# Moving two weight loads and one due date in a fused attention and double MLP kernel

## The chip, the cores and the metric

The kernel runs on one core of a Trainium2 chip. The metric is the device time of one execution in microseconds (us), the median of several runs. Engines are named as in the profile: PE (TensorE) multiplies matrices, with PEld for its weight loads; DVE is VectorE, ACT is ScalarE, POOL is GpSimd, and SP is SyncE, which here only issues transfers. A transfer (DMA) is issued by SP or POOL, in the order of that engine's queue, and moved by 16 shared DMA engines.

## The reference

Three stages follow each other on 6016 tokens with 256 channels, all in float32.

```python
qn = q / (norm(q, axis=tokens) + 1e-6);  kn = k / (norm(k, axis=tokens) + 1e-6)
a  = softmax(kn.T @ qn / tau)             # 256 x 256, over channels
x  = v @ a                                # 6016 x 256
h  = x @ w1;  x = (h * sigmoid(1.702 h)) @ w2      # d_ff 2048
h  = x @ w3;  y = where(h > 0, h, exp(min(h, 0)) - 1) @ w4
```

## The kernel before, in words

A first phase reads q and k, sums up `kn.T @ qn` and takes the softmax. The matrix `a` is folded into the first weights, so that `x @ w1` needs v alone; the fold of w1 is done in four parts on PE (`fold_w1`), the first ahead of the main loop and the other three during it.

The main loop has two passes. Pass A is the first MLP and pass B the second. Each pass runs over six groups of tokens (five of 1024 and one of 896), and each group over eight units, one for 256 of the 2048 hidden columns. A unit is written (pass, group, unit), all counted from 0: (A,0,0) is the first of the 96. Its first product is done by a Strassen-like scheme with seven products, numbered 1 to 7 and issued in the order 1, 5, 6, 2, 7, 3, 4 (line L678). Each of the seven is three matmuls, because every float32 number is kept as a high and a low part. So a unit has 21 matmuls for its first product and 24 (L776) for its second product, which belongs to the unit before it: the second product of unit u is issued among the first products of unit u+1. ACT and DVE stand between the two: ACT copies one sum from bank to bank near the unit's start (L945, awaited by product 6) and another (L952), DVE adds (L956, awaited by product 7, and L966, awaited by product 4), and both compute the activation and its high and low parts (L708, L709, L741).

Beside this runs background work, in one list called `queue`. Each unit has eight places (`bg(0)` to `bg(7)`) where a step or two of it is issued: in group 0 of pass A 1, 2, 1, 2, ... steps, 12 in all, in the later groups of pass A one at each place. In that list stand:

- the conversion of the weights (`rounds`, `some`). A block of 512 columns is loaded raw, scaled by ACT (L202, L203: two passes), shifted, joined and given its sign by DVE (L207, L210, L213), and split into a high part by ACT (L245) and a low part by DVE (L251). The blocks go through in the order of the list `order`: w1 0, w1 1, w2 0, w1 2, w1 3, w2 1, w2 2, w1 4, w1 5, w2 3, w2 4, w1 6, w1 7, w2 5, w2 6, w2 7. They are staggered: round t scales block t+1 and ends block t-2 in its first step, joins block t and splits off the high part of block t-1 in its second, gives block t its sign in the third and shifts block t+1 in the fourth. `some(12, near)` takes twelve steps and goes on to the end of the round. w3 and w4 follow as `far`, and their results are stored to DRAM (`w3d`, `w4d`).
- the last parts of the folded w1 (`combine_w1`, six steps, L264 and L267 to L275),
- the turning of v for the next group (`blocks_v`, L378, two steps for each half of the group; the second half's load, sixteen small transfers on SP at L371, is issued when the first half is done),
- the operands of the next group of a pass (`operands`): seven operands, each made by ACT (L425) and DVE (L416, L429) and stored to DRAM by POOL (L431) in tiles that share four buffers, so that the last of the seven needs the buffer of the third.

`need(name, i)` forces steps of the conversion until block i is done, at the place where it is called. Before the change it is called at the start of unit (A,0,p) for w2 block p. The second product of unit (A,0,p) reads that block, and that product is issued in the unit that follows.

At the last unit of a group, each product is followed by `load_next`, which reloads the operand that the product has just read for the last time (L131, on SP). It does so only if the operands of the next group are marked as made; the mark is set for all seven at once at the end of `operands`. What isn't loaded then is loaded at the unit's end.

In the last group of pass A (group 5) the weights of pass B are loaded on SP at the ends of units: the first weights in four parts c (L1078, 1792 KB each) over the first weights of units 2c and 2c+1 of pass A, and the second weights p-1 (L1081, 512 KB each) over those of unit p-1. SP takes its instructions in the order written; each waits until the buffer's last reader on PE is done.

Ahead of the main loop the list `PACE1` takes 16 steps of the conversion.

Of the kernel before, what the change touches and what calls it, by code (L numbers as in the profile page):

```python
# [22 lines left out]
def kernel(  # L23
# [47 lines left out]
    NP = KF // 2  # L71
# [39 lines left out]
    XOP = {1: 0, 2: 1, 3: 2, 4: 3, 5: 4, 6: 5, 7: 6}  # L111
# [5 lines left out]
    def first_weights(kind, c):  # L117
        w_first[kind, c] = wts.tile([P, 2, 2, 7, P], F32R, tag=f"wA{c}", name=f"wA{kind}")
        return w_first[kind, c]

    def second_weights(kind, p):
        w_second[kind, p] = wts.tile([P, 2, 2, C], F32R, tag=f"wB{p}", name=f"wB{kind}")
        return w_second[kind, p]

    def x_tile(kind, b, i):
        x_t[kind, b, i] = xp.tile([P, 2, BANK], F32R, tag=f"x{i}", name=f"x{kind}")
        return x_t[kind, b, i]

    def load_x(kind, b, i):
        n = wid[b]  # L130
        nc.sync.dma_start(out=x_tile(kind, b, i)[:, :, :n].bitcast(F32), in_=xd[kind, b][:, i, :, :])  # L131
# [5 lines left out]
    def stage(shape, name):  # L137
        return stg.tile(shape, F32R, tag="st", name=name, bufs=4)
# [200 lines left out]
    def parts(n, work=near):  # L339
        while n:  # L340
            x = next(work, None)
            if x is None:
                return
            n -= not x

    def need(name, i):
        while state["done"] < place[name, i]:
            n = place[name, i]
            parts(1, near if n < NEAR - 1 else last_near if n < NEAR else far)
# [37 lines left out]
    made = set()  # L387
# [18 lines left out]
    def operands(kind, b, direct=False):  # L406

        n = wid[b]
        t = full.pop((kind, b))
        b11, b12 = (t[:, 0, i * n:(i + 1) * n] for i in range(2))  # L410
        b21, b22 = (t[:, 1, i * n:(i + 1) * n] for i in range(2))
        temp = {}

        def sub(i, x, y):
            temp[i] = stg.tile([P, BANK], F32, tag="t", name="tt", bufs=3)
            nc.vector.tensor_sub(temp[i][:, :n], x, y)  # L416

        def tgt(i):
            if direct:
                return x_tile(kind, b, i)  # L420
            return stage([P, 2, BANK], "xt")

        def hi(i, x):
            d = hold_t[i] = tgt(i)
            nc.scalar.copy(d[:, 0, :n], x)  # L425

        def lo(i, x):
            d = hold_t[i]
            nc.vector.tensor_sub(d[:, 1, :n], x, d[:, 0, :n].bitcast(F32))  # L429
            if not direct:  # L430
                nc.gpsimd.dma_start(out=xd[kind, b][:, i, :, :], in_=d[:, :, :n].bitcast(F32))  # L431

        hold_t = {}
        hi(0, b11)
        sub(4, b12, b11)
        yield False
        hi(1, b21)
        lo(0, b11)
        yield False
        hi(2, b22)  # L440
        lo(1, b21)
        yield False
        hi(4, temp[4][:, :n])
        sub(5, b22, temp[4][:, :n])
        yield False
        lo(2, b22)
        lo(4, temp[4][:, :n])
        yield False
        hi(5, temp[5][:, :n])
        sub(6, b22, b12)  # L450
        yield False
        hi(6, temp[6][:, :n])
        lo(5, temp[5][:, :n])
        yield False
        sub(3, b21, temp[5][:, :n])
        lo(6, temp[6][:, :n])
        yield False
        hi(3, temp[3][:, :n])
        yield False
        lo(3, temp[3][:, :n])  # L460
        made.add((kind, b))
        yield False
# [40 lines left out]
    with tc.manual_schedule():  # L503
        make_identity(nc, ident)

        with ExitStack() as st:
# [24 lines left out]
            for i, m in enumerate(CHUNKS):  # L531
# [22 lines left out]
                if i in (8, 9):  # L554
                    if i == 8:
                        full_tile("A", 0)
                    for c in range(KC):
                        transpose_v(0, i - 8, c, bank[4 + 2 * (i - 8) + c])
                    if i == 9:
                        v_ops = operands("A", 0, direct=True)  # L560
                elif i > 9:
                    parts([1, 1, 1, 0][i - 10], v_ops)
# [19 lines left out]
            for i in range(2):  # L582
                for c in range(KC):
                    x = i * KC + c
# [72 lines left out]
        loaded = set()  # L657

        def load_next(u, i):

            if u[2] < NP - 1 or u not in units[:-1]:
                return
            nxt = units[units.index(u) + 1][:2]
            if nxt in made and nxt + (i,) not in loaded:
                loaded.add(nxt + (i,))
                load_x(*nxt, XOP[i])

        def product(dst, i, u, start):
            product_(dst, i, u, start)
            load_next(u, i)  # L670
# [197 lines left out]
        def finish(kind, b):  # L868
            while (kind, b) not in made:
                background(1)  # L870
# [141 lines left out]
        def v_later(b, h):  # L1012
            if h == 0:
                if b > 1:
                    finish("B", b - 2)
                full_tile("A", b)
                queue.insert(1, blocks_v(b, 0))
            else:
                queue.insert(1, chain(blocks_v(b, 1), operands("A", b)))

        def some(n, work):

            safe = False
            while n > 0 or not safe:
                safe = next(work, None)
                if safe is None:
                    return
                if not safe:
                    n -= 1
                    yield  # L1030
# [10 lines left out]
        for b in range(NG):  # L1041
            if b + 1 < NG:
                plan_at(("A", b, 1), lambda b=b: load_v(b + 1, 0))
                plan_at(("A", b, 3), lambda b=b: v_later(b + 1, 0))
                plan_at(("A", b, 5), lambda b=b: v_later(b + 1, 1))
            nxt = units[units.index(("A", b, 7)) + 2]
            plan_at(nxt, lambda b=b: queue.append(operands("B", b)))

        for t in range(len(units) + 1):
            u = units[t] if t < len(units) else None  # L1050
            if u:
                kind, b, p = u
                if kind == "A" and b == 0 and p:
                    need("w2", min(p, NP - 1))
                if u == ("B", 0, 0):
                    passA.close()
                    tp = ctx.enter_context(tc.tile_pool(name="tpB", bufs=1))
                for f in plan.get(u, []):
                    f()
                if kind == "A":  # L1060
                    if b == 0:
                        queue.append(some(12, near) if p < 5 else some(12, last_near))
                    if b and p % 2 == 0:
                        queue.append(some(1, far))
            step(t)
            if u is None:
                break

            if p == NP - 1:
                nxt = units[t + 1] if t + 1 < len(units) else None  # L1070
                if nxt:
                    finish(*nxt[:2])
                    for i in (1, 5, 6, 2, 7, 3, 4):
                        load_next(u, i)
            if kind == "A" and b == NG - 1:
                if p % 2:
                    c = p // 2
                    nc.sync.dma_start(out=first_weights("B", c).bitcast(F32), in_=w3d[c])  # L1078
                if p:
                    need("w4", p - 1)  # L1080
                    nc.sync.dma_start(out=second_weights("B", p - 1).bitcast(F32), in_=w4d[p - 1])  # L1081
                if p == NP - 1:
                    need("w4", p)
            if u == ("B", 0, 0):
                nc.sync.dma_start(out=second_weights("B", NP - 1).bitcast(F32), in_=w4d[NP - 1])
# [29 lines left out]
```

## Time and profile before

| | us |
|---|---|
| median of 3 runs (lowest to highest) | 1082.22 (1078.76 to 1082.24) |
| the profiled execution | 1078.05 |
| its span | 1076.3 |
| PE busy | 1047.0 (97%) |
| DVE busy | 840.7 (78%) |
| ACT busy | 759.6 (71%) |
| POOL busy | 72.1 (7%) |
| mean DMA rate | 134 GB/s over 144.31 MB |

The times inside the span are counted from its start. Pass A's main loop runs from about 67 to 573 us, pass B from there to the end. In a row of a timeline the number ahead is the start, the next the length, and the bracket at the end tells how long the engine was idle before it and what ended that. `x6` is the number of instructions merged into the row. Matmuls overlap, so that the distance of two starts tells their rate and not the length of one. The granted clock is a share of 2.4 GHz; it has two levels, 1.2 and 2.4 GHz.

### The profile page before, as it was taken

Reading aid. Unit: us, or ns where it says so; the run is one execution under the profiler, and the core shown is the slowest. Engines: PE = TensorE matmul, PEld = TensorE weight load, DVE = VectorE, ACT = ScalarE, POOL = GpSimd, SP = SyncE. Lnnn points to the kernel's source line nnn. Section 1 sums busy time; section 2 is a strip of 40 time slices with the busy share of each in tenths; the row PEclk is TensorE's granted clock in tenths of the full one; section 3 lists DMA queues with packets and bytes.
Section 4 is the critical chain, followed back from the end, with each engine's and each line's share of the span. In section 5 each row is a group of like instructions: output and inputs, shape, how many; then the busy total and the mean of one; then the engine's idle time right before and its main releaser. Section 6 shows DMA issues by size and latency. Waiting matters only on the chain.

```text
span 1076.3 us, 13797 instructions
## 1 busy us (share of the span) xinstructions
PE 1047.0 (97%) x4808; PEld 873.5 (81%) x4808; DVE 840.7 (78%) x1366; ACT 759.6 (71%) x1423; POOL 72.1 (7%) x126
## 2 busy tenths in 40 slices
PE   8989989999999999999899999999999999999998
PEld 6867868888888888888798877887888788788897
DVE  5987785677776785675436999988998998989986
ACT  5778777667777777766557776777676777777675
POOL 0000010012211220120100100000000000000000
PEclk9999999999999999999999999999999999999999
DMA  9913255358548557535746124104204204203200
GB/s 341 371 41 77 59 184 193 116 186 280 195 176 286 199 184 253 171 139 178 270 176 259 43 78 151 25 1 144 32 1 138 38 1 137 40 1 120 40 1 35
DMA packets 124918, 144.31 MB, mean 134 GB/s; under 512 B 90224, under 2 KB 94416, under 8 KB 124336
## 3 DMA queue, kind: packets, MB, share of 16 engines
q1 hardware_dynamic: 108704, 84.05, 25.6%
q0 software_dynamic: 16144, 59.38, 14.9%
q8 instruction: 38, 0.62, 0.2%
q14 instruction: 32, 0.26, 0.1%
HBM read 86.25 MB, written 57.15 MB: 133 GB/s over the span
## 4 chain that ended last, share of the span: by engine, by line
PE 61%; issue 16%; DVE 12%; ACT 5%; POOL 3%; DMA 3%; SPq 0%; DVEq 0%; POOLq 0%; ACTq 0%
PE b L678 28%; PE b L776 28%; PE b L800 4%; DVE gg L730 2%; DVE ee L725 2%; DVE sq L523 1%; DVE g L741 1%; DMA qk<-in_k_dram 1%; DVE ob L834 1%; DMA xdB<-xt 1%; PE b L474 1%; POOL xdA L431 1%; ACT g L737 1%; POOL xdB L431 1%; DVE b L956 1%
## 5 line engine op out<-in xcount | busy, mean ns | idle before, releaser
L776 PE MATMUL b<-g,wBA 128*128 128x512 f32 (+1 forms) x1152 | 296.6, 386 | 1.7 <-DVE g L741 1.7
L678 PE MATMUL b<-xA,wAA 128*128 128x512 f32 (+1 forms) x1008 | 267.8, 389 | 9.7 <-ACT b L945 4.5
L678 PE MATMUL b<-xB,wAB 128*128 128x512 f32 (+1 forms) x1008 | 265.3, 387 | 1.9 <-DVE b L956 1.9
L776 PE MATMUL b<-g,wBB 128*128 128x512 f32 x960 | 252.3, 390 | 2.9 <-ACT g L737 1.8
L776 PEld LDWEIGHTS b<-g,wBA 128*128 128x128 f32 x1152 | 216.9, 188 | 42.9 <-DVE g L741 2.2
L678 PEld LDWEIGHTS b<-xA,wAA 128*128 128x128 f32 x1008 | 188.5, 189 | 50.7 <-ACT b L945 8.4
L678 PEld LDWEIGHTS b<-xB,wAB 128*128 128x128 f32 x1008 | 186.3, 188 | 40.0 <-DVE b L956 4.6
L776 PEld LDWEIGHTS b<-g,wBB 128*128 128x128 f32 x960 | 179.8, 188 | 43.4 <-ACT g L737 3.9
L737 ACT CAST g<-gg 128x512 fp32r<-128x512 f32 (+1 forms) x192 | 117.9, 614 | 114.2 <-DVE gg L730 110.1
L725 DVE SCALAR_TENSOR_TENSOR ee<-ee,th 128x512 f32<-128x512 f32 (+1 forms) x192 | 129.5, 674 | 28.2 <-ACT th L715 28.2
L708 ACT ACTIVATE g<-b 128x512 fp32r<-128x512 f32 (+1 forms) x144 | 84.9, 590 | 87.8 <-PE b L678 87.2
L956 DVE TENSOR_TENSOR b<-b,s 128x512 f32<-128x512 f32 (+1 forms) x96 | 65.9, 687 | 100.9 <-PE b L678 93.5
L741 DVE TENSOR_TENSOR g<-gf,g 128x512 fp32r<-128x512 f32 (+1 forms) x192 | 128.5, 674 | 16.0 <-ACT gf L709 15.8
L741 DVE TENSOR_TENSOR g<-gg,g 128x512 fp32r<-128x512 f32 (+1 forms) x192 | 129.4, 674 | 8.9 <-ACT g L737 4.4
L730 DVE SCALAR_TENSOR_TENSOR gg<-b,ee 128x512 f32<-128x512 f32 (+1 forms) x144 | 98.0, 681 | 5.0
L714 ACT ACTIVATE ee<-b 128x512 f32<-128x512 f32 (+1 forms) x144 | 84.4, 586 | 21.7 <-PE b L678 21.6
L709 ACT ACTIVATE gf<-b 128x512 f32<-128x512 f32 (+1 forms) x144 | 84.4, 586 | 2.9 <-DVE g L741 2.5
L966 DVE TENSOR_TENSOR c<-b,s 128x512 f32<-128x512 f32 (+1 forms) x96 | 64.7, 674 | 24.4 <-PE b L678 24.2
L715 ACT ACTIVATE th<-b 128x512 f32<-128x512 f32 (+1 forms) x144 | 83.8, 582 | 0.0
L952 ACT COPY s<-b 128x512 f32<-128x512 f32 (+1 forms) x96 | 56.2, 586 | 21.4 <-PE b L678 21.4
L945 ACT COPY b<-b 128x512 f32<-128x512 f32 (+1 forms) x96 | 56.0, 583 | 16.9 <-PE b L678 16.8
L565 PE MATMUL b<-qk 128*128 128x256 f32 x188 | 43.8, 391 | 5.4 <-DMA qk<-in_k_dram 5.2
(101 smaller groups left out, 840.8 us busy)
## 6 DMA issues: line engine op xcount, KB each, us to landing
xdB<-xt POOLq DMA_DIRECT2D x35, 512.0 KB, 3.5
xB<-xdB SPq DMA_DIRECT2D x35, 512.0 KB, 5.2
xdA<-xt POOLq DMA_DIRECT2D x28, 512.0 KB, 3.2
xA<-xdA SPq DMA_DIRECT2D x28, 512.0 KB, 6.3
wAB<-w3d SPq DMA_DIRECT2D x4, 1792.0 KB, 7.8
out_dram<-ob SPq DMA_DIRECT2D x160, 32.0 KB, 1.6
qk<-in_q_dram SPq DMA_DIRECT2D x9, 512.0 KB, 5.8
qk<-in_k_dram SPq DMA_DIRECT2D x9, 512.0 KB, 6.7
```

Of the source, the lines that this page charges most:

```text
L678: nc.tensor.matmul(dst[:, :n], w[:, wi, p % 2, WOP[i], :], x[:, xi, :n], start=(start and k == 0), stop=(k == 2), skip_group_check=True,)
L708: nc.scalar.activation(self.sl(ik)[0], h, AF.Gelu_apprx_sigmoid)
L709: nc.scalar.activation(t[:, :n], h, AF.Gelu_apprx_sigmoid)
L714: nc.scalar.activation(e[:, :n], h, AF.Exp)
L715: nc.scalar.activation(t[:, :n], h, AF.Tanh, scale=0.5)
L725: nc.vector.scalar_tensor_tensor(out=e[:, :n], in0=e[:, :n], scalar=1.0, in1=t[:, :n], op0=ALU.add, op1=ALU.mult,)
L730: nc.vector.scalar_tensor_tensor(out=g[:, :n], in0=h, scalar=0.0, in1=e[:, :n], op0=ALU.max, op1=ALU.min)
L737: nc.scalar.copy(self.sl(ik)[0], self.tmp[ik][:, :self.n])
L741: nc.vector.tensor_sub(lo, self.tmp.pop(ik)[:, :self.n], hi.bitcast(F32))
L776: nc.tensor.matmul(bank[a][:, :n], w[:, f, wi, d * P:(d + 1) * P], g[:, gi, k * n:(k + 1) * n], start=fresh((kind, b, a)), stop=(p == NP - ...
L956: nc.vector.tensor_add(bank[c][:, :n], bank[b][:, :n], s5[:, :n])
L966: nc.vector.tensor_add(c22[:, :n], bank[b][:, :n], s5[:, :n])
```

## The change

Three things are changed. The loads of pass B's first weights, until now at the ends of units 1, 3, 5 and 7 of pass A's last group, stand at the ends of units 3, 4, 5 and 7, each still ahead of that unit's load of second weights. An operand is marked as made as soon as its own store is issued, and `load_next` asks for the mark of that operand alone; the mark for the whole group stays. And w2 block p is due at the start of unit p+1 of group 0 and no longer at that of unit p; the last block is due at unit (A,1,0).

```diff
@@ operands: lo @@
             if not direct:
                 nc.gpsimd.dma_start(out=xd[kind, b][:, i, :, :], in_=d[:, :, :n].bitcast(F32))
+                made.add((kind, b, i))
@@ load_next @@
             nxt = units[units.index(u) + 1][:2]
-            if nxt in made and nxt + (i,) not in loaded:
-                loaded.add(nxt + (i,))
-                load_x(*nxt, XOP[i])
+            x = nxt + (XOP[i],)
+            if x in made and x not in loaded:
+                loaded.add(x)
+                load_x(*x)
@@ the loop over the units @@
                 if kind == "A" and b == 0 and p:
-                    need("w2", min(p, NP - 1))
+                    need("w2", p - 1)
+                if u == ("A", 1, 0):
+                    need("w2", NP - 1)
@@
             if kind == "A" and b == NG - 1:
-                if p % 2:
-                    c = p // 2
+
+                for c in {3: (0,), 4: (1,), 5: (2,), 7: (3,)}.get(p, ()):
                     nc.sync.dma_start(out=first_weights("B", c).bitcast(F32), in_=w3d[c])
```

## Rows read from the trace of the kernel before

**Rows 1.** The page's busy shares: busy us, share of the span, instructions.

```profile
PE 1047.0 (97%) x4808; PEld 873.5 (81%) x4808; DVE 840.7 (78%) x1366; ACT 759.6 (71%) x1423; POOL 72.1 (7%) x126
```

**Rows 2.** Busy time by stretch: pass A's first group and its fifth.

```profile
core 0: us, PE busy (x) PEld busy (x) DVE busy (x) ACT busy (x) POOL busy (x), PEclk, DMA share, GB/s
...
68.50:167.00 98.50, 91.03 (x393) 72.18 (x392) 78.52 (x140) 74.38 (x140) 5.77 (x10) 0.98 0.38 114
412.80:494.60 81.80, 81.80 (x361) 67.47 (x360) 54.56 (x90) 58.01 (x111) 12.43 (x20) 1.00 0.55 184
```

**Rows 3.** Timeline of PE at the start of unit (A,0,1).

```profile
77.88 0.73 PE L776 MATMUL b<-g,wBA 128*128 128x512 f32 x2 [1.73 <-DVE g L741]
...
79.14 0.84 PE L776 MATMUL b<-g,wBA 128*128 128x512 f32 x3
82.19 2.62 PE L678 MATMUL b<-xA,wAA 128*128 128x512 f32 x6 [2.20 <-ACT b L945]
```

**Rows 4.** Busy time by stretch, columns as in rows 2: around two long stops.

```profile
82.10:86.30 4.20, 4.11 (x11) 3.26 (x12) 2.79 (x6) 2.15 (x5) 0.00 (x0) 0.59 0.67 167
...
523.40:526.50 3.10, 3.02 (x9) 2.70 (x10) 2.41 (x5) 2.93 (x7) 0.84 (x2) 0.53 1.03 420
...
511.60:526.40 14.80, 11.72 (x51) 10.10 (x50) 9.13 (x16) 8.74 (x18) 3.20 (x6) 0.88 1.00 375
```

**Rows 5.** Timeline of ACT at the start of unit (A,0,1).

```profile
80.39 0.71 ACT L202 ACTIVATE raw<-raw 128x512 f32<-128x512 f32 x1
...
81.50 0.63 ACT L945 COPY b<-b 128x512 f32<-128x512 f32 x1
```

**Rows 6.** Timeline of PE: its other stops in pass A's first group.

```profile
107.92 1.67 PE L678 MATMUL b<-xA,wAA 128*128 128x512 f32 x6 [0.70 <-ACT b L945]
...
137.82 1.66 PE L678 MATMUL b<-xA,wAA 128*128 128x512 f32 x6 [0.95 <-DVE b L956]
...
146.47 1.66 PE L678 MATMUL b<-xA,wAA 128*128 128x512 f32 x6 [0.61 <-ACT b L945]
...
152.83 0.96 PE L678 MATMUL b<-xA,wAA 128*128 128x512 f32 x3 [0.60 <-DVE c L966]
...
158.53 1.66 PE L678 MATMUL b<-xA,wAA 128*128 128x512 f32 x6 [0.64 <-ACT b L945]
```

**Rows 7.** Timeline of DVE at the start of unit (A,0,5).

```profile
136.46 0.71 DVE L378 STREAM_TRANSPOSE vt<-v_raw 128x512 f32<-128x512 f32 x1 [5.51 <-DMA v_raw<-in_v_dram]
```

**Rows 8.** Timeline of SP: the sixteen loads of v's second half.

```profile
126.06 8.61 SPq L371 DMA_DIRECT2D v_raw<-in_v_dram  x16
```

**Rows 9.** Timeline of SP: the reloads of operands in unit (A,0,7).

```profile
155.88 9.42 SPq L131 DMA_DIRECT2D xA<-xdA  x7
```

**Rows 10.** Timeline of SP: pass B's first weights 0, second weights 0 and 1.

```profile
511.65 0.34 SPq L1078 DMA_DIRECT2D wAB<-w3d  x1
512.86 14.34 SPq L1081 DMA_DIRECT2D wBB<-w4d  x2
```

**Rows 11.** Timeline of POOL: stores of pass B's operands.

```profile
512.17 1.14 POOL L431 DMA_DIRECT2D xdB<-xt  x2 [1.74 <-DVE xt L429]
...
523.18 0.53 POOL L431 DMA_DIRECT2D xdB<-xt  x1 [6.93 <-DVE xt L429]
```

**Rows 12.** Timeline of ACT in unit (A,5,2).

```profile
521.54 0.62 ACT L425 CAST xt<-tt 128x512 fp32r<-128x512 f32 x1 [5.56 <-DMA xdB<-xt]
```

**Rows 13.** Timeline of PE in unit (A,5,2).

```profile
518.11 1.38 PE L678 MATMUL b<-xA,wAA 128*128 128x448 f32 x6
519.32 1.38 PE L776 MATMUL b<-g,wBA 128*128 128x448 f32 x6
523.48 1.49 PE L678 MATMUL b<-xA,wAA 128*128 128x448 f32 x3 [2.77 <-DVE c L966]
```

**Rows 14.** The page's transfers: KB each, median us to landing.

```profile
xdB<-xt POOLq DMA_DIRECT2D x35, 512.0 KB, 3.5
```

**Rows 15.** Busy time by stretch, columns as in rows 2: unit (A,0,4).

```profile
120.30:130.30 10.00, 10.00 (x45) 8.16 (x45) 9.96 (x18) 6.92 (x14) 1.28 (x2) 1.00 0.30 74
```

## Prediction

> **What bounds the kernel now.** I read the page's busy shares first, then the busy time stage by stage, then TensorE's own timeline in the stages that are not full. PE is busy 97% of the span [rows 1]: only what leaves holes in PE, or slows its clock, can be won. By stages PE is packed in the middle groups of pass A: in the fifth, 81.80 us of 81.80 [rows 2], so one 512-column matmul costs 81.80 / 361 = 0.227 us. In the first group it is busy 91.03 of 98.50 us [rows 2]. Pass A's last group has one large hole [rows 13].
>
> First group. PE stops 1.73 us at 77.88 and 2.20 us at 82.19 [rows 3]. Each stop costs some 0.17 us more than its idle time: three matmuls from 79.14 end at 79.82, and the next starts at 82.19, 2.37 late. Behind the second stop the granted clock is 0.59 for 4.20 us [rows 4], most of it at 1.2 of 2.4 GHz, which costs 0.41 x 4.20 = 1.72 us. Five smaller stops follow, 0.70, 0.95, 0.61, 0.60 and 0.64 us idle [rows 6], with the 0.17 each 4.35 us. Three wait for ScalarE's copy at L945 at the start of a unit, two for VectorE.
>
> Last group of pass A. At 511.65 SP issues the 1792 KB load of pass B's first weights 0, and just behind it a 512 KB load [rows 10]; POOL stores operands for pass B from 512.17 [rows 11]. The DMA share from 511.60 to 526.40 is 1.00 [rows 4], and ScalarE, which needs the buffer of an operand stored at 512.17, stands 5.56 us until 521.54 [rows 12], where such a store lands in 3.5 us in the median [rows 14]. VectorE queues behind that cast, and PE, due at 519.32 + 6 x (519.32 - 518.11) / 6 = 520.53, starts at 523.48 [rows 13]: 2.95 late. Clock 0.53 for 3.10 us [rows 4] adds 1.46. Sum 4.4 us.
>
> **The change, part by part.** *First weights.* Load 0 moves from the end of unit 1 to the end of unit 3, load 1 from 3 to 4; 2 and 3 stay. On SP the order becomes second weights 0, 1, first weights 0, second weights 2, first weights 1, ... . Load 0's buffer was last read in unit 1, so it waits for nothing but its place: it leaves SP right behind second weights 1, now near 512.86 + 14.34 = 527.2 [rows 10], some 4.4 sooner without the hole, near 522.8. The operand store now at 523.18 [rows 11] would by then be out for 5 us (ScalarE's wait of 5.56 is gone), so nothing that a compute engine awaits meets the load. Its first reader is pass B's unit 0, at about 573. Behind it on SP stand 512 KB loads that wait for PE themselves; an issue costs 0.34 us [rows 10]. What is left beside the stores is one 512 KB load. Gain 4.4; the bounds are 0 (the store is late for its own reasons) and 4.4, and I take 4.4, because every other store of the kind, the median of 35, needs 3.5 us.
>
> *Each operand reloaded once stored.* Counted along the queue, a group's operands are all marked in unit 6 in every group, in the first in the fourth of the unit's eight background places; the trace agrees: seven reloads leave SP in 9.42 us from 155.88 [rows 9], one behind each product of the first group's last unit. Marking each one sooner then changes no instruction. PE is full across the later seams [rows 2]. Cost 0, bounds 0 and 0; if an operand were late, the reload would only wait behind fewer others.
>
> *w2 due one unit on.* Conversion of the weights goes in steps. Before unit 0 the pace list takes 16, unit 0 takes 12, together 28. Block n (in the order list) is done at step 4n + 11: w2 block 1 is n = 5, step 31. So at the start of unit 1 steps 29 to 31 are forced, among them both ScalarE passes on the next block, which run from 80.39 to 81.50, just ahead of the copy that PE waits for [rows 5]. With block 0 due instead (n = 2, step 19) nothing is forced. All later dates are met in both versions, so the rest of the first group runs three steps behind; no operation is added.
> - Unit 1: the copy comes 81.50 - 80.39 = 1.11 us sooner; the stop shrinks from 2.20 to 1.09. The clock held through the idle 1.73 and fell after 2.20 [rows 3, 4], so I expect it to hold: 1.72 more (bounds 0 and 1.72; the nearer row is 1.73, after which it held).
> - Start of unit 3 (107.92): two ScalarE passes, 1.11 us, leave the end of unit 2 for the start, where ScalarE idles. 0.87 goes.
> - Unit 5 (137.82): VectorE stands 5.51 us for v [rows 7], because the transposes come ahead of the addition at L956 and v's sixteen loads, from 126.06, take 8.61 us to issue [rows 8]. Now the first transposes end one place sooner and the next come behind L956, ahead of L966, whose product PE ends only 24 matmuls (3 of product 2, two folds of 6, 6 of the unit before, 3 of product 7) = 5.4 us later. 1.12 goes.
> - Unit 6: operand work comes two places later. At 146.47 ScalarE has the same two casts but starts sooner: 0.4 of 0.78. At 152.83 VectorE has one operation (0.6) less ahead of L966: 0.6 of 0.77.
> - Start of unit 7 (158.53): the last w2 cast leaves the place ahead of the copy: 0.81 goes.
> - Against it: the end of unit 3 gets one cast more (0.62, the length of a cast in [rows 12]) ahead of a ScalarE copy without slack: 0.5 lost, bounds 0 and 0.8. VectorE gets about 0.9 more in unit 4, where it is busy 9.96 of 10.00 us [rows 15]; the idle 5.51 right behind covers that, and 0.9 is the price without the cover.
>
> Moved with it: v's first sixteen loads now go ahead of a raw w2 block on SP, some 9 us [rows 8] on a block wanted two units later: nothing.
>
> Sum: first group -1.1 - 1.7 - 0.9 - 1.1 - 0.4 - 0.6 - 0.8 + 0.5 = -6.1 (bounds +1.7 and -7.2: the two prices just named with nothing gained, or all of these stops gone with the clock held); last group of A -4.4; together -10.5. The profiled execution took 1078.05 (span 1076.3 and 1.75 around it), so 1067.5 on its scale. The median shown is 1082.22 with runs from 1078.76: on that scale 1071.7. I say 1070, between the two.
>
> One rule of the Trainium skill speaks against the first part. Rows first: beside the load of 1792 KB a 512 KB store needs until 521.5, 9.4 us [rows 11, 12]. The page "DMA: Bandwidth & Descriptors", section "Queues, rings and completion order", says that each DMA engine takes turns between the queue rows it has work for, packet by packet. With equal turns that store would have landed after about twice its own time and not behind the whole load, so the load would not be the whole cause; the row does not look like equal turns. By the rule the hole would stay, which is the third rival below.
>
> **The rivals.**
> 1. The first group gives back little: its stops change places, since ScalarE and VectorE do the same work in the same units (VectorE 9.96 of 10.00 in unit 4 [rows 15]), and the clock falls once anyway. For it: seven stops of different makes; against: ScalarE is busy only 74.38 of 98.50 [rows 2]. Gain 4.4 + 1.1 = 5.5, less up to 1.5 of new stops: 1073 to 1078 over both scales, 1075 in the middle.
> 2. Nothing: load 0 falls on something in units 2 to 4 and the first group is even. 1078 to 1082.
> 3. The store is late of its own, through POOL's queue or its writes, not through the load. The hole of 4.4 stays: -6.1, so 1072 to 1076. Against it is the saturated DMA in just that stretch [rows 4].
> 4. Slower. VectorE's wait for v now stands ahead of L966, and the operands for the second group finish two places later. It decides if v lands after PE's seventh product in unit 5, so that the 5.51 us [rows 7] stand open, the clock falls (1.72), and the operands are not all marked when unit 7 begins: then the reloads, 9.42 us for seven [rows 9], go at the group's end in full view. 5.5 + 1.7 + 9.4 = 16.6, less 1.1 paid already and less 4.4 + 2.8 gained: +8.3, 1086 to 1090. Against: the work ends in the sixth place of unit 6, two places and a unit's start before.
>
> **How the numbers follow.** Forecast 0.60 (gain of 7.5 to 12: 1066 to 1075 over both scales), rival 1 0.20, rival 2 0.05, rival 3 0.10, rival 4 0.05. A change under 0.5%, 5.4 us, can't be told from none here. Faster by more: the forecast whole, half of rival 1 and 0.06 of rival 3, 0.76. Slower by more: rival 4, 0.05. The same: 0.19. The range runs from 1065.5, just under every term at its bound (-7.2 - 4.4 from 1078.05 is 1066.4), to 1078, where only the last group's term is left on the median's scale; beyond it are rivals 2 and 4 and a tenth of the rest.
>
> **What would show it.** Right: no wait of ScalarE for an operand store in pass A's last group, PE full there and its clock at 1.00; the load of first weights 0 issued near 522; in the first group no half clock in unit 1, a stop of about 1.1 us at its first copy, no VectorE wait ahead of L956 in unit 5. Wrong: PE's busy time in the first group's window not above 91 of some 93 us; a wait of PE on first weights in pass B; a half clock at a new place; SP's seven reloads at another time than during unit 7.

## The result and the profile after

The changed kernel takes 1070.47 us in the median of four runs (1069.65 to 1071.9), the kernel before on the same chip 1081.38 (1078.76 to 1082.24): a ratio of 0.9918 [0.9899, 0.9938]. This ratio, like those below, is an estimate of its own with a 95% interval and not the quotient of the two medians, which is 0.9899 and lies at the interval's lower end; by the ratio the gain is 8.9 us, by the medians 10.9. The forecast was 1070 and faster. The profiled execution took 1070.31 us, its span 1068.5. In the code after the change the lines of the main loop stand two lower (L678 is L680, L945 is L947, L966 is L968) and the two loads of weights four lower (L1082, L1085).

Busy time by stretch in the kernel after: pass A's first group, its four middle groups, its last group, pass B. The columns are those of [rows 2].

```profile
69.70:163.10 93.40, 88.96 (x393) 71.27 (x392) 78.31 (x140) 74.53 (x141) 5.77 (x10) 1.00 0.37 112
163.10:491.30 328.20, 327.92 (x1441) 269.85 (x1440) 227.94 (x380) 235.86 (x447) 54.59 (x91) 1.00 0.60 201
491.30:565.40 74.10, 74.00 (x362) 67.57 (x361) 37.40 (x63) 45.07 (x94) 4.81 (x9) 1.00 0.61 222
565.40:1068.50 503.10, 493.32 (x2325) 412.35 (x2323) 447.02 (x704) 360.28 (x688) 5.00 (x7) 1.00 0.22 63
```

The same view of the kernel before, for the three stretches that [rows 2] does not have whole:

```profile
167.00:494.60 327.60, 327.57 (x1441) 270.02 (x1441) 227.89 (x380) 235.91 (x447) 54.60 (x91) 1.00 0.59 199
494.60:573.20 78.60, 75.52 (x362) 68.54 (x361) 37.51 (x63) 45.09 (x94) 4.81 (x9) 0.98 0.57 210
573.20:1076.30 503.10, 493.43 (x2325) 412.39 (x2323) 447.00 (x704) 360.31 (x688) 5.00 (x7) 1.00 0.22 63
```

The numbers of instructions agree stretch by stretch to within one, so nothing was added or removed; only idle time and clock differ. The first group is 5.1 us shorter, the last one 4.5, the middle 0.6 longer, pass B the same, and the main loop starts 1.2 later (69.7 against 68.5). That makes the 7.8 by which the two spans differ. The later start is not the change's: in the nine profiles of the experiments, whose first phase is the same, the first product of the main loop starts anywhere from 66.5 to 70.2 us (before 66.3, after 67.5). Without it the stretches give 9.0. The medians differ by 10.9: the profiled execution of before lies 3.3 under its median, that of after 0.2.

**The last group.** Timelines of the kernel after, in turn SP, POOL, ACT and PE:

```profile
509.57 9.82 SPq L1085 DMA_DIRECT2D wBB<-w4d  x2
519.45 0.60 SPq L1082 DMA_DIRECT2D wAB<-w3d  x1
```

```profile
508.88 1.13 POOL L431 DMA_DIRECT2D xdB<-xt  x2 [1.74 <-DVE xt L429]
```

```profile
512.37 0.63 ACT L425 CAST xt<-tt 128x512 fp32r<-128x512 f32 x1
```

```profile
515.83 1.38 PE L778 MATMUL b<-g,wBA 128*128 128x448 f32 x6
517.05 0.77 PE L680 MATMUL b<-xA,wAA 128*128 128x448 f32 x3
```

They answer to [rows 10 to 13]. The store is out at 508.88, and the cast that needs its buffer goes at 512.37 with no bracket behind it: ScalarE waited for nothing. PE goes from one product into the next, 515.83 + 1.22 = 517.05, where before it stood 2.77 us. The first weights 0 leave SP at 519.45, or 522.75 on the clock of before (this group starts at 491.3 there 494.6); the prediction had 522.8.

**The first group.** PE's stops after, of 0.2 us and more; they answer to [rows 3, 6]:

```profile
79.08 0.73 PE L778 MATMUL b<-g,wBA 128*128 128x512 f32 x2 [1.74 <-DVE g L743]
...
82.28 1.65 PE L680 MATMUL b<-xA,wAA 128*128 128x512 f32 x6 [1.10 <-ACT b L947]
...
118.90 1.66 PE L680 MATMUL b<-xA,wAA 128*128 128x512 f32 x6 [0.27 <-ACT b L947]
...
143.05 1.67 PE L680 MATMUL b<-xA,wAA 128*128 128x512 f32 x6 [0.61 <-ACT b L947]
...
154.59 1.66 PE L680 MATMUL b<-xA,wAA 128*128 128x512 f32 x6 [0.68 <-ACT b L947]
...
170.76 0.94 PE L680 MATMUL b<-xA,wAA 128*128 128x512 f32 x3 [0.23 <-DMA xA<-xdA]
```

The stop at unit 1's copy went from 2.20 to 1.10. Those that stood at 107.92, 137.82 and 152.83 are gone, a small one of 0.27 came at the end of unit 3, those of units 6 and 7 (146.47 and 158.53 before) are still there, and a new one waits for a reloaded operand in (A,1,0). Behind the stop of 1.10 the clock stayed at 2.4 GHz (ahead of this, as [rows 4], 0.59):

```profile
82.00:90.00 8.00, 7.72 (x34) 6.39 (x35) 4.04 (x8) 6.06 (x13) 0.00 (x0) 1.00 0.41 67
```

### The profile page after: what moved, and what is told of

It is laid out like the page before. It is cut to its first block, busy times and chain, and to the rows that moved or that the text cites. A ratio compares the mean times of both kernels' runs of the same rounds, so it can differ in the third digit from the quotient of the medians.

```text
span 1068.5 us, 13795 instructions
## 1 busy us (share of the span) xinstructions
PE 1044.9 (98%) x4808; PEld 873.0 (82%) x4808; DVE 840.5 (79%) x1366; ACT 759.6 (71%) x1423; POOL 72.1 (7%) x126
## 4 chain that ended last, share of the span: by engine, by line
PE 80%; DVE 9%; ACT 5%; DMA 4%; issue 1%; SPq 1%; DVEq 0%; ACTq 0%
PE b L778 37%; PE b L680 37%; PE b L802 4%; DMA qk<-in_k_dram 2%; DVE gg L732 2%; DVE ee L727 2%; PE b L566 1%; DVE ob L836 1%; DVE g L743 1%; DMA xA<-xdA 1%; ACT g L739 1%; DMA v_raw<-in_v_dram 1%; PE b L475 1%; DVE b L958 1%; ACT gf L711 1%
## 5 line engine op out<-in xcount | busy, mean ns | idle before, releaser
L680 PE MATMUL b<-xA,wAA 128*128 128x512 f32 (+1 forms) x1008 | 266.0, 387 | 4.0 <-ACT b L947 2.7
L680 PE MATMUL b<-xB,wAB 128*128 128x512 f32 (+1 forms) x1008 | 265.2, 387 | 2.0 <-DVE b L958 2.0
L680 PEld LDWEIGHTS b<-xA,wAA 128*128 128x128 f32 x1008 | 187.8, 188 | 44.2 <-ACT b L947 6.8
L680 PEld LDWEIGHTS b<-xB,wAB 128*128 128x128 f32 x1008 | 186.2, 188 | 40.0 <-DVE b L958 4.7
L958 DVE TENSOR_TENSOR b<-b,s 128x512 f32<-128x512 f32 (+1 forms) x96 | 66.0, 687 | 100.2 <-PE b L680 90.8
L968 DVE TENSOR_TENSOR c<-b,s 128x512 f32<-128x512 f32 (+1 forms) x96 | 64.7, 674 | 23.6 <-PE b L680 23.3
L947 ACT COPY b<-b 128x512 f32<-128x512 f32 (+1 forms) x96 | 56.0, 584 | 17.2 <-PE b L680 17.1
```

Of the source, the lines that this page charges most:

```text
L680: nc.tensor.matmul(dst[:, :n], w[:, wi, p % 2, WOP[i], :], x[:, xi, :n], start=(start and k == 0), stop=(k == 2), skip_group_check=True,)
L958: nc.vector.tensor_add(bank[c][:, :n], bank[b][:, :n], s5[:, :n])
L968: nc.vector.tensor_add(c22[:, :n], bank[b][:, :n], s5[:, :n])
```

## The experiments

**Each edit alone.** Three kernels on one chip, where the kernel before has a median of 1079.66. First the weights:

```diff
-                if p % 2:
-                    c = p // 2
+                for c in {3: (0,), 4: (1,), 5: (2,), 7: (3,)}.get(p, ()):
                     nc.sync.dma_start(out=first_weights("B", c).bitcast(F32), in_=w3d[c])
```

> Of the three edits only the first: the loads of pass B's first weights stand at the ends of units 3, 4, 5 and 7; the mark and w2's due dates are as before. If the load of 1792 KB is what delays the operand stores, the hole of 2.95 us and the 1.46 us of half clock behind it in unit (A,5,2) go and nothing else moves: 4.4 of 1080, a ratio of 0.996; the load of first weights 0 leaves SP near 523, right behind second weights 1, and ScalarE waits under 1 us for the store's buffer. If the gain of the whole change came from w2's due dates alone, 1.000 and the hole stays. If the store is late of its own, 1.000 as well, with the wait of 5.6 us still there and the load elsewhere.

1074.77 us (1074.15 to 1076.45), ratio 0.9951 [0.9933, 0.9968], 4.9 less. The hole and the half clock of the last group are gone and the first group's stops are as before. PE's second stop in the first group is as long as before, and the clock holds behind it (timeline and stretch of this kernel):

```profile
84.41 1.66 PE L678 MATMUL b<-xA,wAA 128*128 128x512 f32 x6 [2.20 <-ACT b L945]
```

```profile
84.30:88.60 4.30, 4.19 (x18) 3.49 (x19) 2.98 (x6) 3.31 (x8) 0.00 (x0) 1.00 0.66 161
```

So the half clock that I read in [rows 4] does not belong to that stop in every execution.

The mark alone:

```diff
+                made.add((kind, b, i))
...
-            if nxt in made and nxt + (i,) not in loaded:
...
+            x = nxt + (XOP[i],)
+            if x in made and x not in loaded:
...
```

> Only the second edit: each operand is marked as made when its own store is issued. If all operands were marked in unit 6 anyway, every engine's instructions come in the order of before, and the ratio is 1.000 within 0.002. If reloads go out sooner, SP's seven reloads leave before unit 7 or earlier within it, and the gain is up to 0.5 us a group, 2 us in all: 0.998.

1079.55 us (1077.73 to 1081.81), ratio 0.9995 [0.9982, 1.0009]. Every engine has the same instructions in the same order as before. The hole is there (2.62 us idle), and so are the first group's stops.

The date of w2 alone:

```diff
-                    need("w2", min(p, NP - 1))
+                    need("w2", p - 1)
+                if u == ("A", 1, 0):
+                    need("w2", NP - 1)
```

> Only the third edit: w2 block p due at the start of unit p+1. If the stop at the first copy of unit (A,0,1) falls from 2.2 to 1.1 us idle because two ScalarE passes leave its place, and the clock holds through the shorter stop, the first group gives back 4 to 5 us (1.1 + 1.7 there, the rest in its later stops) and the last group's hole stays with its half clock: a ratio of 0.996. If the half clock of unit 1 has nothing to do with the stop's length, it comes again and the gain is 2.5: 0.998. If the stops only change places, 0.999 to 1.000.

1075.66 us (1075.0 to 1077.38), ratio 0.9962 [0.9943, 0.9981], 4.0 less by the medians; the interval reaches from 2.1 to 6.2. The first group's stops are those of the changed kernel (the one of unit 6 did not show in this execution); ScalarE stands 5.36 us for the store, and the last group's hole is still whole:

```profile
520.60 0.87 PE L678 MATMUL b<-xA,wAA 128*128 128x448 f32 x3 [2.57 <-DVE c L966]
```

The edits add up: 0.9951 x 0.9995 x 0.9962 = 0.9908, and the whole change is 0.9918.

**Why the store was late.** The forecast took it that the running load holds the store up. Three kernels vary the load and leave the rest as before. The first puts load 0 at the end of unit 2:

```diff
-                if p % 2:
-                    c = p // 2
+                for c in {2: (0,), 3: (1,), 5: (2,), 7: (3,)}.get(p, ()):
```

> Before, with the load of first weights 0 written at the end of unit 2 instead of unit 1, ahead of second weights 1 and so right behind second weights 0 in SP's queue; nothing else changed. If the place in SP's queue sets the time and not the unit, it leaves near 513.2, 1.5 us later than before and 10 us ahead of unit 2's end. Then two answers: if a load hinders the store by all the bytes that it has under way, the 1792 + 512 KB are under way as before and the hole stays, 2 to 3 us with half clock: 0.999 to 1.000. If it is by the size of its packets (in the trace of before 14336 bytes each for first weights, 4096 for second weights and for the stores, and the stores' queue moves nothing while the large ones run), the awaited store shares only with second weights 0, lands near 516.5, and the hole goes: 0.996. If the unit named sets the time, the load leaves near 523 and the ratio is 0.996 too.

1075.59 us (1073.87 to 1076.06), ratio 0.9949 [0.9929, 0.997]: the same gain as from unit 3. Timelines of SP, POOL and ACT:

```profile
515.15 0.34 SPq L1080 DMA_DIRECT2D wBB<-w4d  x1
515.54 0.75 SPq L1077 DMA_DIRECT2D wAB<-w3d  x1
```

```profile
514.47 1.13 POOL L431 DMA_DIRECT2D xdB<-xt  x2 [1.74 <-DVE xt L429]
```

```profile
517.95 0.62 ACT L425 CAST xt<-tt 128x512 fp32r<-128x512 f32 x1
```

The load goes only 1.1 us behind the awaited store, and the store still lands in 3.4 us (517.88). The store's packets run from 515.6 to 517.2, and those of the load begin at 519.0, behind the 512 KB of second weights 0, which were issued between the two. What counts is that the store was out first. The stores behind it then needed 10.5 to 11.9 us, and nobody waited for those. From 519 to 525 the two queues moved nearly the same number of packets (q1 is SP's, q0 POOL's; packets, MB, share of the 16 engines):

```profile
q1 hardware_dynamic: 151, 1.78, 77.9%
q0 software_dynamic: 157, 0.59, 24.1%
```

Next, load 0 where it was, but as four transfers of 448 KB:

```diff
+                    t = first_weights("B", c)
+                    if c == 0:
+                        for x in range(2):
+                            for h in range(2):
+                                nc.sync.dma_start(
+                                    out=t[:, x, h].bitcast(F32), in_=w3d[c][:, x, h]
+                                )
...
```

> Before, with the load of first weights 0 in its old place at the end of unit 1, but cut into four loads of 448 KB, so that its packets are 3584 bytes each and no longer 14336; the same bytes at the same place. If the size of the packets makes the store late (with 14336-byte packets under way, the awaited store's first packet came some 4 us after its issue, and from then on the two queues moved packet for packet), the awaited store lands 4 to 5.5 us after its issue, ScalarE waits 0 to 1.5 us, and the hole goes with its half clock: 0.996. If the bytes ahead of the store count, whatever their packets, 1792 + 512 KB are still there, the store lands 8 us or more after its issue, and the hole stays at 2 us or more: 0.999 to 1.000.

1075.21 us (1072.3 to 1076.9) against 1080.13, ratio 0.9954 [0.9935, 0.9974]. The store, out at 513.96, landed at 520.97, 7.0 us, between the answers expected. ScalarE's wait is shorter and PE's hole is a sixth of the 2.77 of before, with no half clock:

```profile
521.05 0.62 ACT L425 CAST xt<-tt 128x512 fp32r<-128x512 f32 x1 [3.24 <-DMA xdB<-xt]
```

```profile
522.98 0.87 PE L678 MATMUL b<-xA,wAA 128*128 128x448 f32 x3 [0.46 <-DVE c L966]
```

Its transfers by queue tell of two phases. From 515.0 to 517.6 only SP's queue moves anything:

```profile
q1 hardware_dynamic: 182, 0.60, 85.6%
```

From 518.5 to 521.0 POOL's has its turns:

```profile
q0 software_dynamic: 175, 0.65, 63.6%
q1 hardware_dynamic: 122, 0.40, 39.1%
```

The kernel before has the same two, from 513.0 to 516.9, and from 517.0 to 520.0:

```profile
q1 hardware_dynamic: 85, 1.22, 90.8%
q0 software_dynamic: 1, 0.00, 0.0%
```

```profile
q1 hardware_dynamic: 93, 0.65, 61.7%
q0 software_dynamic: 99, 0.41, 32.8%
```

To tell a silence of fixed length from one that ends with the load, load 0 was cut in two, and only its first half left where it was, 896 KB; the other half follows at the end of unit 3:

```diff
-                if p % 2:
+                if p == 1:
+                    t0 = first_weights("B", 0)
+                    nc.sync.dma_start(out=t0[:, 0].bitcast(F32), in_=w3d[0][:, 0])
+                elif p % 2:
                     c = p // 2
+                    if c == 1:
+                        nc.sync.dma_start(out=t0[:, 1].bitcast(F32), in_=w3d[0][:, 1])
```

> Before, with half of the load of first weights 0 (896 KB, packets of 7168 bytes) left at the end of unit 1 and the other half moved to the end of unit 3, just ahead of the load of first weights 1. In the kernel before and with the load in four pieces alike, the awaited store moved nothing for about 4 us after its issue and then went packet for packet beside the load. If that silence goes with the bytes of the load that lie ahead of it, it is near 2 us now, the store lands 5 to 6 us after its issue, ScalarE waits 1 to 2 us and PE's hole is under 0.3 us with no half clock: 0.995 to 0.996. If the silence is a fixed cost of starting a store beside a load, it is 4 us again, the store lands 7 to 8 us after its issue, and the hole is 0.6 to 1.5 us.

1074.66 us (1073.52 to 1076.05) against 1078.1, ratio 0.9968 [0.9952, 0.9984]. The store went out at 513.42 and landed at 520.74, 7.3 us, and PE stood 0.78:

```profile
520.82 0.62 ACT L425 CAST xt<-tt 128x512 fp32r<-128x512 f32 x1 [3.57 <-DMA xdB<-xt]
```

```profile
522.75 0.87 PE L678 MATMUL b<-xA,wAA 128*128 128x448 f32 x3 [0.78 <-DVE c L966]
```

Half the bytes in the way, and the store is as late as with all of them in smaller pieces, as the second of the two answers had it. From 515.0 to 517.3 POOL's queue moved nothing, from 517.3 to 517.5 three packets. So from issue to first packet it was 3.9 us here, 4.8 in the kernel before (512.17 to 517.0) and 4.3 with four parts (513.96 to 518.3): the silence changes far less than the load's size, while the turns behind it do change. Nor does it end with the load: in the kernel before, of the packets of SP's queue between 517.0 and 517.5, twelve of 0.17 MB, all are still of the load's 14 KB. A store with no load ahead of it has 1.1 us of it: in the kernel before, the first operand's store goes out at 508.92 and its first packet at 510.0, and the awaited store of the changed kernel does the same at 508.88 and 510.0. So 2.8 to 3.7 us of the silence come with the load. What makes them stays open.

**The stops that stayed.** In the kernel before, the last w2 cast stood ahead of unit 7's copy, which went at 157.88 (timeline of ACT):

```profile
156.38 0.62 ACT L245 CAST wBA<-bits 128x512 fp32r<-128x512 f32 x1 [0.96 <-DVE bits L213]
```

In the changed kernel that cast goes behind the copy (154.91), and ScalarE has the two passes on the last w2 block ahead of it instead, with no idle time from 150.80 to the copy:

```profile
150.80 0.68 ACT L202 ACTIVATE raw<-raw 128x512 f32<-128x512 f32 x1
151.36 0.67 ACT L203 ACTIVATE raw<-raw 128x512 int32<-128x512 uint32 x1
...
153.91 0.62 ACT L947 COPY b<-b 128x512 f32<-128x512 f32 x1
```

Two kernels were made from the changed one and run with it on one chip. The first starts the last round of the conversion one unit later:

```diff
-                        queue.append(some(12, near) if p < 5 else some(12, last_near))
+                        if p < 5:
+                            queue.append(some(12, near))
+                        elif p == NP - 1:
+                            queue.append(some(12, last_near))
```

> The changed kernel, with the conversion of the last w2 block held back to unit (A,0,7) (its steps enter the list at unit 7 and no longer at units 5 and 6; it is due at unit (A,1,0) as before). If the stop of 0.84 us at the start of unit 7, which I had expected to go, is made by the two ScalarE passes of that block standing ahead of the copy, it goes, and nothing else changes by more than 0.2: 0.7 to 0.9 us under the changed kernel on the same chip, a ratio to before near 0.991. If it is made by the late stores of the operands (ScalarE waits for their buffers in unit 6), it stays and the ratio is that of the changed kernel.

1068.75 us (1067.93 to 1070.88), ratio to before 0.99 [0.9883, 0.9916]. It has the lowest median of all, though its interval overlaps with that of the changed kernel below. The passes now follow the copy:

```profile
153.42 0.59 ACT L947 COPY b<-b 128x512 f32<-128x512 f32 x1
...
154.41 0.67 ACT L202 ACTIVATE raw<-raw 128x512 f32<-128x512 f32 x1
```

The stops of unit 7 and of the reload are gone. ScalarE's wait for an operand store's buffer, 0.43 us in unit 6, is the same in both kernels, so the late stores alone did not make the stop of unit 7. PE's stops in the first group of this kernel:

```profile
79.80 0.73 PE L778 MATMUL b<-g,wBA 128*128 128x512 f32 x2 [1.74 <-DVE g L743]
83.02 1.65 PE L680 MATMUL b<-xA,wAA 128*128 128x512 f32 x6 [1.12 <-ACT b L947]
119.62 1.66 PE L680 MATMUL b<-xA,wAA 128*128 128x512 f32 x6 [0.28 <-ACT b L947]
143.51 1.67 PE L680 MATMUL b<-xA,wAA 128*128 128x512 f32 x6 [0.47 <-ACT b L947]
```

The changed kernel once more, beside it:

> The changed kernel itself, beside the others on the same chip: 0.990 to 0.994. It tells whether the three edits alone, 0.9951, 0.9995 and 0.9962, add up (0.9908), and whether the half clock in unit (A,0,1) stays away a second time with the stop at 1.1 us idle; with the stop of 2.2 us it came in two of four profiled executions so far. If the clock there is chance, it can come here too.

1071.09 us (1069.29 to 1072.71), ratio 0.9919 [0.9901, 0.9936]. The first two stops are there again (1.73 and 1.07 us idle, with no half clock behind the second), so is the 0.28 at the end of unit 3, and the one of unit 6 did not show. The other two, at unit 7 and at the reload:

```profile
155.42 1.65 PE L680 MATMUL b<-xA,wAA 128*128 128x512 f32 x6 [0.66 <-ACT b L947]
169.66 0.96 PE L680 MATMUL b<-xA,wAA 128*128 128x512 f32 x3 [0.33 <-DMA xA<-xdA]
```

The medians differ by 2.3 us where the two stops are worth 0.66 + 0.33 and 0.17 each, 1.3; the remaining 1.0 is less than either kernel's runs spread (3.0 and 3.4 us), and its cause stays open.

The second, on top of that, issues one step and no longer two at every other place of unit 0:

```diff
-                    background(2 if u[1] == 0 and i % 2 else 1)
+                    background(2 if u[1] == 0 and u[2] and i % 2 else 1)
```

> As the run with the last w2 block in unit 7, and unit (A,0,0) takes 8 background steps in place of 12. ScalarE is packed in that unit, so the two stops behind it (1.74 and 1.10 us idle in the changed kernel) should shrink with the one scaling (1.1) and the one cast (0.6) that leave the unit: 1.5 to 2.5 us less there. Against it, two conversion steps are forced in unit 1 ahead of the fold (0.3 to 0.6), and the next group's operands are stored some six places later, so that PE may wait for a reload in unit (A,1,0), 0 to 2 us. I expect 1 us under the run before it, a ratio near 0.990; if the reloads decide, 1 us above it.

1070.62 us (1070.2 to 1072.96), ratio 0.9919 [0.99, 0.9937], 1.9 over the median of the kernel that it was made from. The first stop shrank from 1.74 to 0.34, the second did not (1.15), and three others came, the last three here:

```profile
76.29 0.74 PE L778 MATMUL b<-g,wBA 128*128 128x512 f32 x2 [0.34 <-DVE g L743]
79.55 1.65 PE L680 MATMUL b<-xA,wAA 128*128 128x512 f32 x6 [1.15 <-ACT b L947]
92.16 0.50 PE L778 MATMUL b<-g,wBA 128*128 128x512 f32 x1 [0.98 <-DVE wBA L251]
105.11 1.66 PE L680 MATMUL b<-xA,wAA 128*128 128x512 f32 x6 [0.86 <-ACT b L947]
154.22 2.93 PE L680 MATMUL b<-xA,wAA 128*128 128x512 f32 x6 [2.23 <-ACT b L947]
```

The steps not done in unit 0 are done later. At 92.16 PE waits for a block of w2 that is not ready. Ahead of the last and longest of these stops ScalarE stood 2.25 and 0.86 us for the buffers of operand stores, so that its copy came late; that stop has a half clock behind it as well (0.60 for 4.3 us). The reload in (A,1,0), which I had feared, made no stop.

## Why the prediction came out right, step by step

- **Last group, -4.4.** Right: -4.5 by stretches, -4.9 by the edit alone. The third rival, a store late of its own, fell with the first experiment: the hole goes when the load moves. (That every other store of the kind needs 3.5 us was read wrongly from a median: the three right behind the awaited one needed 10.7 to 11.2.) But my picture of why, a store that has to wait until the whole load is through, is only half right. It stands through a silence and after that takes turns with the load. The page "DMA: Bandwidth & Descriptors" of the Trainium skill, section "Queues, rings and completion order", has the turns packet by packet, and from 517 on the trace agrees (93 packets to 99). I had read equal turns as equal shares of the time, and from that the third rival. But the load's packets are 14336 bytes and the store's 4096: from 517.0 to 519.0, 44 packets of the store were 0.18 MB and 38 of the load 0.48 MB. So turns, too, make a store late beside such a load, and that the hole would stay when the load moves did not follow. It went because the awaited store landed before the load was issued (512.26 and 519.45 in the kernel after).
- **Mark, 0.** Right: 1.0 in ratio within 0.0018, and every engine's instructions kept their order.
- **First group, -6.1.** By stretches -5.1, by the edit alone -4.0 (interval -2.1 to -6.2). Of its terms, as idle time:
  - unit 1's copy, 1.09 expected, 1.10 measured; units 3 and 5 (the stops at 107.92 and 137.82) gone; 152.83 gone; the new stop at the end of unit 3, 0.5 expected, 0.27 idle and so 0.44 with the 0.17 of a stop.
  - Unit 5 went as told: VectorE's wait for v is now 3.35 us, stands ahead of L968 and no longer of L958, and PE doesn't notice. The size of the term was from one profile: in the six profiles with the old date that stop was 0.41 to 1.45 us idle.
  - Unit 6 (146.47), 0.4 of 0.78 expected, nothing gained in the changed kernel's profile. VectorE's wait for v in unit 5 was 3.35, 3.12, 2.68 and 2.52 us in four profiles of the new due date, and this stop 0.61, 0.47, none and none: it seems to go with the arrival of v, which is not shown, since no run changed v's loads alone.
  - Unit 7 (158.53), -0.8 expected, nothing gained (0.64 before, 0.68 after): **the step that failed**. I took the last w2 cast out of the place ahead of the copy and did not see what slides into it from three steps behind, two scaling passes of the last block, 1.12 us (150.80 to 151.92). The kernel that converts that block one unit later shows it: there they go behind the copy and the stop is gone.
  - Not foreseen: the wait for a reloaded operand in (A,1,0), 0.23 to 0.33. It is gone in the same kernel, where the seven reloads take at most 7.8 us to land; in the changed kernel it is up to 9.6, before up to 7.0. What slows them stays open.
  - The clock, -1.7. I made it a fixed effect of the stop. With the stop of 2.2 the half clock came in two of six profiles (before, and load 0 at unit 2) and with the stop of 1.1 in none of five. That is worth 1.7 x 2/6 = 0.6 in the mean, if the shorter stop never has it, which five profiles don't settle. What decides it stays open.
  
  In the two profiles, where the kernel before had its half clock, that makes -6.1 + 0.4 + 0.8 = -4.9 against -5.1. For the edit alone, with the clock at its mean (1.1 less), it makes -3.8 against -4.0; the profile of that kernel has no stop at the reload. The interval of -4.0 is too wide to tell -3.8 from -6.1, so this account rests on the stops in the profiles.
- **The sum, -10.5.** The first pair of medians gives -10.9; two others give -9.0 (1080.13 to 1071.09, and the single edits, -4.9 - 0.1 - 4.0). The ratio gives -8.9, and the stretches without the later start -9.0. By these the sum was 1.5 too large: in the stretches 1.0 of it lies in the first group and 0.6 in the middle ones, where I had put nothing and the stop at the reload is 0.4 with its 0.17; the last group gave 0.1 more. The forecast's 1070 stood between the two scales, and a sum of -9.0 from 1079.66, the median of before beside the single edits, would have said 1070.7. That 1070 came within 0.5 of the measured median is in part luck: the choice of scale made up for what the sum had too much.
- **A sign of mine that was badly set.** I called it wrong if PE's busy time in the first group were not above 91 of some 93 us. It is 88.96 of 93.40, and the prediction's mechanism held all the same. The 91.03 of before had matmuls at half clock in it, which count as busy for longer; the idle time is what to compare, 7.47 before and 4.44 after.
- **The slower case** did not come: the seven reloads go out in 9.46 us from 151.90, in unit 7 as before. The first rival was right in kind about a little: what left unit 7 was replaced, and two small stops came, 0.44 at unit 3 and 0.40 at the reload. But it left the first group a gain of 1.1 at most, and the edit alone gave at least 2.1 by its interval; and the clock did not fall. PE waited for no first weights in pass B.

## What to carry to other kernels

Put a long load behind, not ahead of, a transfer that an engine is about to wait for: being issued 0.5 us behind such a load or 1.1 ahead of it (with a 512 KB load between the two) decided between 9.3 and 3.4 us to landing. When a due date in a staggered pipeline moves, go through every place where the old steps stood and ask what moves into it; here the steps removed ahead of a waited-for copy were replaced by others. And a drop of the clock seen in one profile is a chance, not a price: look at several before it goes into a sum.

## What was not expected of the hardware

- A 512 KB store that was issued on POOL's queue 0.5 us behind a load on SP's moved nothing for 4.8, 4.3 and 3.9 us, with the load 1792 KB whole, in four parts, and halved; it landed after 9.3, 7.0 and 7.3 us. Issued 1.1 us ahead of the same load it had its first packet after 1.1 and landed after 3.4.
- Once turns are taken they are by packet, and bytes go by packet size: 157 packets of the stores were 0.59 MB while 151 of the loads were 1.78 MB in the same 6 us.
- The granted clock is not a function of the stop: 2.19 to 2.23 us idle at the same place in the same order of work gave 0.59 in two executions and 1.00 in four. Ahead are the first group's [rows 4] and the stretch of the kernel with the weights alone; the other half clock, with load 0 at unit 2:

```profile
84.80:89.00 4.20, 4.18 (x11) 3.31 (x12) 2.89 (x6) 2.09 (x4) 0.00 (x0) 0.59 0.67 162
```
